# Which engine closes a one-core kernel: the gather, the semaphore clear and the last wait moved from GpSimd and SyncE to VectorE

## The chip, the cores and the metric

The kernel runs on 1 core of one Trainium2 chip. The metric is device time in microseconds (us) of one execution; medians of several runs are given. A program on one core has no second die to compare with. Unless said otherwise, the runs below are in the state that the measurements call fast; one run of the kernel before took 745.57 us, was marked slow, and is left out everywhere.

## The reference

A gated sum of two blocks for one token. Block A is grouped-query attention over a cache of 65,536 positions (32 query heads, 4 key/value heads, 128 wide), block B is a small gated MLP. Cut to what matters:

```python
q = (x @ wq).reshape(1, 1, 32, 128).transpose(0, 2, 1, 3)
k, v = jnp.repeat(k_cache, 8, axis=1), jnp.repeat(v_cache, 8, axis=1)
p = softmax(einsum('bhqd,bhkd->bhqk', q, k) * 128 ** -0.5)
a = einsum('bhqk,bhkd->bhqd', p, v).transpose(0, 2, 1, 3).reshape(1, 1, 4096) @ wo
# ... b = the MLP block ...
return g * a + (1 - g) * b            # g = sigmoid(sum(x * gate_w))
```

Only the size of the caches matters here: two times 67 MB of bfloat16 are read once. The change does not touch the arithmetic.

## The kernel before

The body streams the caches and weights through one buffer with DMAs on SyncE's queue, computes under them, and ends with one copy on ScalarE and two output DMAs, one issued by ScalarE and one by SyncE:

```python
    # ... all loads, attention, projection ...
    nc.scalar.copy(out=out_sb[:], in_=out_ps[:])
    for i, queue in enumerate((nc.scalar, nc.sync)):
        p0 = (2 * i + 1) * B - 1
        ins = queue.dma_start(out=out_rows[2 * i:2 * i + 2, :], in_=out_sb[p0:p0 + 2, :])
        out_queues.append(ins.ins.name)
```

GpSimd computes only at the start (index tables, ones, two zeroed weight buffers), until about 5 us. The framework appends a closing block, and the kernel has already cut it down in a hook that edits the finished program:

```python
    def close_with_one_barrier(n):
        block = n.main_func.blocks[-1]
        # ... `by`: the block's instructions by engine ...
        for engine, l in by.items():
            kinds = [k for _, k, _ in l]
            if engine == mybir.EngineType.Pool:                   # GpSimd
                # ... assert: Drain, wait (gather), add (release), Drain, clear, Drain, 2 more ...
                drop += [l[2][0], l[6][0], l[7][0]]
                closer, gather = l[0][0], l[1][2]
                continue
            if engine == mybir.EngineType.SP:                     # SyncE
                # ... take over and drop its wait for everything ...
                l, kinds = l[1:], kinds[1:]
            assert kinds == ["InstDrain", "InstEventSemaphore"] * 2
            drop += [l[1][0], l[2][0]]
            if engine == mybir.EngineType.SP:
                closed = l[3][0]
            else:
                drop.append(l[3][0])
        # ... the output DMAs count on a semaphore of their own, `landed`;
        #     `closer` waits for everything else, `closed` waits for `landed` ...
        for i in sorted(drop, reverse=True):
            del block.instructions[i]
```

What is left: PE, ScalarE, VectorE and SyncE each drain and add one to a gather semaphore. GpSimd waits for all other work, for the four signals of the gather, drains, clears the kernel's semaphores with one instruction, and drains again. SyncE then holds the last wait: both outputs have landed.

## Time and profile before

| | before |
|---|---|
| time, median of 3 runs | 382.19 us (382.17 to 382.25) |
| profiled run: time, span of the kernel's own instructions | 382.16 us, 380.7 us |
| bytes moved, DMA rate | 162.17 MB, 426 GB/s |
| GpSimd busy | 4.4 us, all of it before 6 us |

The page of the kernel before: the span, the engines' busy time, and the line of the DMA queue that carries the loads (packets, MB, share of the time of 16 DMA engines).

```profile
span 380.7 us, 2605 instructions
PE 233.2 (61%) x1395; PEld 56.0 (15%) x800; DVE 218.5 (57%) x211; ACT 39.6 (10%) x55; POOL 4.4 (1%) x10
q1 hardware_dynamic: 3892, 162.01, 98.8%
```

No compute engine is busy over 61% of the span, and the load queue fills 98.8% of the DMA engines' time. The kernel is bound by its loads.

The end of the kernel before, from its timeline, weight loads left out (start, duration, engine, line, what; idle time before in brackets):

```profile
378.58 0.29 PE L506 MATMUL out_ps<-kv,oa 128*32 128x256 bf16 x4 [0.35 <-DMA kv<-in_A_wo_dram]
378.92 0.37 ACT L552 CAST out_sb<-out_ps 128x256 bf16<-128x256 f32 x1 [45.10 <-PE out_ps L506]
379.32 0.32 SPq L555 DMA_DIRECT2D out_dram<-out_sb  x1
379.32 0.25 ACTq L555 DMA_DIRECT2D out_dram<-out_sb  x1
```

The issue of the outputs, at 379.32, is the zero of the tables below. The timeline leaves out drains and waits of the sequencers, so the closing block does not show in it. It shows when one asks for the source line that its instructions carry (engine, operation, count; duration in ns as minimum/median/maximum; start of the first and the last; a q marks an engine's sequencer, PEldq that of PE):

```profile
L591 POOLq EVENT_SEMAPHORE  x6: 17/43/682, 376.0 to 379.9; - x6
L591 POOLq DRAIN  x3: 34/41/72, 379.4 to 380.2; - x3
L591 DVEq DRAIN  x1: 345/345/345, 369.6 to 369.6; - x1
L591 PEldq DRAIN  x1: 347/347/347, 378.6 to 378.6; - x1
L591 ACTq DRAIN  x1: 240/240/240, 379.6 to 379.6; - x1
L591 SPq DRAIN  x1: 174/174/174, 379.7 to 379.7; - x1
L591 POOLq EVENT_SEMAPHORE_RANGE_CLEAR  x1: 96/96/96, 380.1 to 380.1; - x1
L591 SPq EVENT_SEMAPHORE  x1: 17/17/17, 380.6 to 380.6; - x1
```

GpSimd (POOLq) gathers at 379.9, clears at 380.1 and begins its last drain at 380.2. SyncE's last wait is over at 380.65. VectorE has drained already at 369.6.

**After the span.** The time of the profiled run, 382.16 us, is longer than the span, 380.7 us. The trace shows no instruction after the span, but it records semaphore updates with their times. On semaphore 2 there are two groups of nine updates; from shortly before the end of the first group until the second, nearly all of the others (246 are recorded in the kernel before) are updated once, in five groups of consecutive numbers (7 to 53, 54 to 104, 105 to 155, 156 to 206, 207 to 255). I read the two groups of nine as barriers and the updates between them as a reset, all three the runtime's, since no instruction in the trace names semaphore 2. These are names for updates: what makes them, and what values they set, is not shown. In the kernel before (us from the span's start):

```
output semaphore, last update 380.619;  SyncE's wait ends 380.653
first barrier   379.178 380.015 380.758 380.802 380.825 | 380.922 380.961 380.995 381.042
reset           380.951 to 381.604
second barrier  381.919 381.953 381.992 382.035 382.058 | 382.157 382.195 382.229 382.276
```

The second barrier takes 382.276 - 381.919 = 0.357 us, in steps of 0.023 to 0.099. The first takes longer: its second to third update needs 0.743 us, where the second barrier needs 0.039. Which engine it waits for there is the question of the experiments.

These updates are tied to the metric: the time of the profiled run equals the sixth update of the second barrier (382.16 and 382.157). So what delays these updates delays the time. Why the time ends at that update is not shown.

### The profile page before, as it was taken

The numbers are of one execution on the slowest core, as the hardware profiler recorded it, in microseconds if no ns is written. First come the engines' busy times: TensorE is split into PE (matmuls) and PEld (weight loads), VectorE is DVE, ScalarE is ACT, GpSimd is POOL, SyncE is SP. The second block draws the span as 40 slices with busy tenths as digits, with TensorE's granted clock in tenths as the row PEclk, the third lists the DMA queues.
The fourth block names the chain that finished last, engine by engine and source line by source line (L and its number), as shares of the span: only waits on it lengthen the run. The fifth ranks groups of instructions, "written<-read, shape, count | busy, mean of one in ns | idle before, by whom it ended". The sixth has DMA issues, their size and how long they took to land.

```text
span 380.7 us, 2605 instructions
## 1 busy us (share of the span) xinstructions
PE 233.2 (61%) x1395; PEld 56.0 (15%) x800; DVE 218.5 (57%) x211; ACT 39.6 (10%) x55; POOL 4.4 (1%) x10
## 2 busy tenths in 40 slices
PE   0060657876157944796397729871977196839386
PEld 0010101111101210111011101120211011202113
DVE  4133288997597506966977059669970388460040
ACT  1001001110601100114010001050100000500000
POOL 4000000000000000000000000000000000000000
PEclk9995769899759895989688958895989579969789
DMA  9998999999999999999999999999999999999995
GB/s 386 496 420 379 411 438 441 437 483 430 387 420 441 441 436 441 427 441 441 434 436 441 441 427 434 406 423 441 434 434 429 420 441 442 436 410 430 424 443 223
DMA packets 3943, 162.17 MB, mean 426 GB/s; under 512 B 472, under 2 KB 476, under 8 KB 860
## 3 DMA queue, kind: packets, MB, share of 16 engines
q1 hardware_dynamic: 3892, 162.01, 98.8%
q8 instruction: 8, 0.13, 0.1%
q14 instruction: 3, 0.02, 0.0%
q10 hardware_dynamic: 40, 0.01, 0.0%
HBM read 162.01 MB, written 0.00 MB: 426 GB/s over the span
## 4 chain that ended last, share of the span: by engine, by line
DMA 57%; PE 26%; DVE 13%; ACT 2%; issue 1%; SPq 1%; DVEq 0%; ACTq 0%
DMA kv<-in_A_k_cache_dram 43%; PE s_ps L410 21%; DMA kv<-in_A_wo_dram 7%; DVE kv L403 7%; DMA kv<-in_A_v_cache_dram 7%; PE o_ps L456 4%; DVE pt L446 2%; DVE o_sb L470 1%; DVE mx L405 1%; ACT sc L421 1%; ACT sc L443 1%; DVE rowt L466 1%; SPq L184 1%; PE om_ps L476 0%; DVE osum L486 0%
## 5 line engine op out<-in xcount | busy, mean ns | idle before, releaser
L410 PE MATMUL s_ps<-kv,wt 128*128 128x512 bf16 x512 | 141.8, 437 | 80.2 <-DVE kv L403 80.2
L403 DVE STREAM_TRANSPOSE kv<-kv 128x2048 int32<-128x2048 int32 x64 | 142.7, 2281 | 54.3 <-DMA kv<-in_A_k_cache_dram 54.3
L456 PE MATMUL o_ps<-kv,pt 128*64 128x512 bf16 x512 | 61.7, 400 | 7.6 <-DMA kv<-in_A_v_cache_dram 7.6
L410 PEld LDWEIGHTS <-wt 128*128 128x128 bf16 x256 | 27.6, 108 | 195.6 <-issue 138.5
L421 ACT CAST sc<-s_ps 128x1024 bf16<-128x1024 f32 x16 | 16.2, 1012 | 249.9 <-PE s_ps L410 249.9
L456 PEld LDWEIGHTS <-pt 128*64 128x64 bf16 x256 | 16.1, 115 | 50.6 <-issue 48.1
L446 DVE STREAM_TRANSPOSE pt<-sc 128x1024 bf16<-128x1024 bf16 x16 | 18.6, 1217 | 6.8 <-ACT sc L443 6.8
L405 DVE TENSOR_REDUCE mx<-sc 128x1 f32<-128x1024 bf16 x12 | 14.5, 1210 | 9.9 <-ACT sc L421 9.9
L443 ACT ACTIVATE sc<-sc,nb 128x1024 bf16<-128x1024 bf16 x16 | 18.2, 1137 | 12.3 <-DVE nb L439 12.2
L466 DVE TENSOR_TENSOR rowt<-o_ps,own 128x1024 f32<-128x1024 f32 x4 | 4.8, 1195 | 24.9 <-PE o_ps L456 24.9
L476 PE MATMUL om_ps<-o_sb,hsel 128*32 128x128 f32 x8 | 2.3, 386 | 18.3 <-DVE o_sb L470 18.3
L425 DVE TENSOR_REDUCE mx<-sc 128x1 f32<-128x1024 bf16 x4 | 4.9, 1220 | 13.6 <-ACT sc L421 13.6
L296 PE MATMUL q_ps<-kv,xT 128*32 128x512 bf16 x64 | 5.6, 527 | 7.2 <-DMA kv<-in_A_wq_dram 7.2
L252 PE MATMUL xb_ps<-xg,spread 8*128 8x256 bf16 x1 | 0.4, 366 | 13.2 <-DMA xg<-in_gate_w_dram 13.2
L470 DVE TENSOR_REDUCE o_sb<-rowt 128x128 f32<-128x1024 f32 x4 | 7.5, 1872 | 0.1
L363 DVE TENSOR_TENSOR rowt<-q_ps,own_b 128x512 f32<-128x512 f32 x2 | 1.3, 686 | 10.8 <-PE q_ps L296 10.8
L296 PE MATMUL z_ps<-kv,xT 128*32 128x448 bf16 x64 | 5.9, 560 | 0.0
L495 PE MATMUL busy_ps<-wt 128*128 128x512 bf16 x23 | 5.8, 381 | 0.1
L506 PE MATMUL out_ps<-kv,oa 128*32 128x256 bf16 x128 | 4.2, 274 | 2.0 <-DMA kv<-in_A_wo_dram 2.0
L256 DVE TENSOR_TENSOR xm<-xb_ps,sel_i 128x128 f32<-128x128 f32 x2 | 0.5, 287 | 8.0 <-PE xb_ps L252 8.0
L552 ACT CAST out_sb<-out_ps 128x256 bf16<-128x256 f32 x1 | 0.4, 372 | 45.1 <-PE out_ps L506 45.1
L296 PEld LDWEIGHTS <-xT 128*32 128x32 bf16 x64 | 2.6, 136 | 14.6 <-issue 14.6
(90 smaller groups left out, 59.3 us busy)
## 6 DMA issues: line engine op xcount, KB each, us to landing
kv<-in_A_k_cache_dram SPq DMA_DIRECT2D x4, 4096.0 KB, 35.4
kv<-in_A_v_cache_dram SPq DMA_DIRECT2D x2, 4096.0 KB, 26.0
kv<-in_B_w_in_dram SPq DMA_DIRECT2D x1, 7168.0 KB, 19.4
kv<-in_A_wo_dram SPq DMA_DIRECT2D x1, 6144.0 KB
kv<-in_B_w_out_dram SPq DMA_DIRECT2D x1, 3584.0 KB
kv<-in_A_wo_dram SPq DMA_DIRECT2D x1, 1024.0 KB
kv<-in_A_wo_dram SPq DMA_DIRECT2D x1, 512.0 KB
kv<-in_A_wo_dram SPq DMA_DIRECT2D x2, 256.0 KB, 28.2
```

The lines of the kernel that those rows point to most:

```text
L296: ins = nc.tensor.matmul(ps[t * B:(t + 1) * B, k * HN:k * HN + n], lhsT=xT[:, i * KH + c:i * KH + c + 1].to_broadcast([P, B]), rhs=w[:, c, ...
L403: nc.vector.transpose(out=kb[:, v * n:(v + 1) * n], in_=kb[:, v * n:(v + 1) * n])
L405: nc.vector.reduce_max(**late.pop())
L410: ins = nc.tensor.matmul(s_ps[:, k * HN:(k + 1) * HN], lhsT=wt[g % 2][:, v, b].rearrange("p a v h -> p (a v h)"), rhs=kx[:, b // 2, b % 2, ...
L421: nc.scalar.copy(out=sct[g, j][:], in_=s_ps[:])
L425: nc.vector.reduce_max(**late.pop())
L443: nc.scalar.activation(out=sct[g, j][:], in_=sct[g, j][:], func=ACT.Exp, scale=SCALE, bias=nb[:, 0:1], accum_out=lss[g][:, j:j + 1])
L446: nc.vector.transpose(out=ptt[g, j][:].rearrange("p c x -> p (c x)"), in_=sct[g, j][:])
L456: ins = nc.tensor.matmul(o_ps[g][hs, e, :], lhsT=ptt[g, j][:, 2 * u:2 * u + 2, :].rearrange("p c x -> p (c x)"), rhs=vx[:, 2 * u + e], sta ...
L466: nc.vector.tensor_tensor(out=om8, in0=o_ps[g][:].rearrange("p e (v d) -> p (e v) d", d=DH), in1=own_8[:].unsqueeze(2).to_broadcast([P, 2 ...
L470: nc.vector.tensor_reduce(out=o_sb[:], in_=om8.rearrange("p x d -> p d x"), axis=AX.X, op=ALU.add)
L495: ins = nc.tensor.matmul(ps[:, :HN], lhsT=w[:, :P], rhs=w[:, :HN], start=True, stop=True, skip_group_check=True)
```

## The change

The intent: VectorE, idle for over nine microseconds by then, should gather, clear and hold the last wait, so that GpSimd's program is over after its set-up work. The hook keeps one of GpSimd's own two last instructions as the last wait, lets SyncE go after its drain, and then swaps GpSimd and VectorE in the closing block.

```diff
-                drop += [l[2][0], l[6][0], l[7][0]]
-                closer, gather = l[0][0], l[1][2]
+                drop += [l[2][0], l[6][0]]
+                closer, gather, closed = l[0][0], l[1][2], l[7][0]
                 continue
             ...
             assert kinds == ["InstDrain", "InstEventSemaphore"] * 2
-            drop += [l[1][0], l[2][0]]
-            if engine == mybir.EngineType.SP:
-                closed = l[3][0]
-            else:
-                drop.append(l[3][0])
+            drop += [l[1][0], l[2][0], l[3][0]]
         ...
         for i in sorted(drop, reverse=True):
             del block.instructions[i]
+        swap = {mybir.EngineType.Pool: mybir.EngineType.DVE,
+                mybir.EngineType.DVE: mybir.EngineType.Pool}
+        for i, ins in enumerate(block.instructions):
+            if ins.engine in swap:
+                block.instructions[i] = copy.replace(ins, engine=swap[ins.engine])
```

## The prediction

> **What bounds the kernel.** The page gives DMA 98.8% of 16 engines' span on the main queue, 426 GB/s; the table by stretches has the DMA engines at 99 to 100% from 0 to 365 us. It streams 162 MB. The change touches none of that: it rewrites only the closing block, after the last load. In the listing of instructions by engine only the semaphore clear moves, from GpSimd to VectorE.
>
> **The end of the kernel before** (timeline, and the closing line's instructions, us from the span's start). The last matmuls run at 378.58, the output copy at 378.92 for 0.37 us, both output DMAs issue at 379.32. ScalarE's closing drain ends at 379.86, SyncE's at 379.87. GpSimd gathers at 379.89, drains, clears the semaphores at 380.08 (0.10 us), and ends its last drain at 380.23. The outputs' landings, in the trace's semaphore records, end at 380.62; SyncE's last wait ends at 380.65, and the span is 380.7. So GpSimd's gather and clear (about 0.35 us) already lie in the shadow of the output landing, which needs about 1.3 us from issue.
>
> **What the change does.** VectorE's last arithmetic ends at about 369.9, so it is free to gather. The waits, gather and clear move to it; it then holds the wait for the outputs. [...] The span therefore stays 380.7.
>
> **Where something can be won or lost.** The time (382.16 in the profiled run) is longer than the span: after it come the runtime's barrier, a semaphore reset and another barrier, which the trace shows as updates only. The first barrier's updates come at 379.18, 380.02, 380.758, 380.802, 380.825, then back to 381.04. I read these as PE, ACT, GpSimd, VectorE, SyncE in turn (an inference: engines start the kernel in the reverse order after the same barrier). If so GpSimd arrives 0.52 us after its last drain and is the one the barrier waited for; SyncE would have been ready about as soon. Freeing GpSimd early takes this away, but VectorE, fourth in turn, then arrives only after the landing: 380.65 plus its own way into the barrier. ScalarE needed 0.16 us for that way, PE 0.23; with 0.1 to 0.2 for VectorE the fifth update comes at 380.78 to 380.88 against 380.825. That is -0.05 to +0.05 us.
>
> **Prediction.** 382.17 us, 8 in 10 between 381.8 and 382.6, a width mostly for run-to-run differences of DMA timing. Faster by over 2%: 0.003. Within 2%: 0.992. Slower by over 2%: 0.005.
>
> **What would show it right or wrong.** Right: the span 380.7 within 0.3; the closing waits, drains and clear appear on VectorE, over by about 380.3; the last instruction is VectorE's wait, at the landing; GpSimd's last instruction is at about 5 us; the third barrier update follows the second at once, and the fourth comes 0.1 to 0.2 us after VectorE's wait. Wrong: VectorE's chain ending after the landing, or its way into the barrier taking 0.3 us or more.
>
> **What would make it wrong.** The order of engines in the barrier, or the cause of the third update's lateness, is other than I read it; the clear costs far more on VectorE than 0.1 us; GpSimd's early end starts something in the runtime that collides with the loads.

## The result

| | before | changed |
|---|---|---|
| median of 6 runs | 382.18 us (381.99 to 382.25) | 382.24 us (382.11 to 382.49) |
| profiled run, time and span | 382.16, 380.7 us | 382.24, 380.8 us |

The ratio is 1.0003, with a 95% interval of 0.999 to 1.0016: the same. A ratio is the mean time of one kernel's fast runs over that of the other's of the same rounds, so it is not quite the ratio of these medians.

The changed kernel's page, the same three lines:

```profile
span 380.8 us, 2607 instructions
PE 231.3 (61%) x1397; PEld 55.6 (15%) x800; DVE 218.5 (57%) x211; ACT 39.6 (10%) x55; POOL 4.4 (1%) x10
q1 hardware_dynamic: 3892, 162.01, 98.8%
```

The load queue's line is the same, and VectorE, ScalarE and GpSimd are as busy as before. PE's busy time is 1.9 us lower, at a granted clock of 0.852 instead of 0.839 in this run; the kernel waits for its loads all the same. The end of its timeline, weight loads left out:

```profile
378.70 0.29 PE L507 MATMUL out_ps<-kv,oa 128*32 128x256 bf16 x4 [0.35 <-DMA kv<-in_A_wo_dram]
379.04 0.37 ACT L553 CAST out_sb<-out_ps 128x256 bf16<-128x256 f32 x1 [45.48 <-PE out_ps L507]
379.44 0.33 SPq L556 DMA_DIRECT2D out_dram<-out_sb  x1
379.44 0.26 ACTq L556 DMA_DIRECT2D out_dram<-out_sb  x1
```

In this run the stream happened to end 0.12 us later. This is the spread that has to be taken out: in the eleven traces of whole kernels, the issue of the outputs falls anywhere from 379.32 to 379.63. The prediction had named one way in which the change could reach the stream, GpSimd's early end. The three traces in which GpSimd ends early have the issue at 379.33, 379.44 and 379.63, the eight others at 379.32 to 379.60, so nothing points to it. The changed closing line:

```profile
L592 DVEq EVENT_SEMAPHORE  x7: 21/50/672, 376.1 to 380.8; - x7
L592 DVEq DRAIN  x3: 10/10/17, 379.5 to 380.3; - x3
L592 POOLq DRAIN  x1: 4111/4111/4111, 1.0 to 1.0; - x1
L592 PEldq DRAIN  x1: 347/347/347, 378.7 to 378.7; - x1
L592 ACTq DRAIN  x1: 241/241/241, 379.7 to 379.7; - x1
L592 SPq DRAIN  x1: 165/165/165, 379.8 to 379.8; - x1
L592 DVEq EVENT_SEMAPHORE_RANGE_CLEAR  x1: 120/120/120, 380.2 to 380.2; - x1
```

All of it now stands on VectorE (DVEq). GpSimd's one closing drain starts at 1.0 us and lasts 4.1 us, until its last memset is done (5.06 us); it then has nothing left. The updates after it:

```
output semaphore, last update 380.743;  VectorE's wait ends 380.791
first barrier   379.389 380.141 380.179 380.967 380.990 | 381.089 381.127 381.161 381.208
second barrier  381.995 382.029 382.068 382.112 382.135 | 382.234 382.272 382.306 382.353
```

Counted from the issue of the outputs, in us:

| | before | changed |
|---|---|---|
| last engine of the gather has cleared and drained | 0.914 (GpSimd) | 0.882 (VectorE) |
| outputs landed | 1.299 | 1.303 |
| last wait ends | 1.333 (SyncE) | 1.351 (VectorE) |
| second update of the first barrier | 0.695 | 0.701 |
| third | 1.438 | 0.739 |
| fourth | 1.482 | 1.527 |
| fifth | 1.505 | 1.550 |
| last update of the second barrier | 2.956 | 2.913 |

The third update came 0.70 us earlier, as it should if GpSimd had been the one that came late. The fourth now waits, and the fifth is 0.045 us later than before. But the last line has the opposite sign: from the end of the first barrier to the start of the second it took 0.877 us in the profile of before and 0.787 in that of the changed kernel. That needed an experiment too.

### The profile page after: what moved, and what is told of

The parts are those of the page before. It is cut to its first block, busy times and chain, and to the rows that moved or that the text cites. A ratio compares the mean times of both kernels' runs of the same rounds, so it can differ in the third digit from the quotient of the medians.

```text
span 380.8 us, 2607 instructions
## 1 busy us (share of the span) xinstructions
PE 231.3 (61%) x1397; PEld 55.6 (15%) x800; DVE 218.5 (57%) x211; ACT 39.6 (10%) x55; POOL 4.4 (1%) x10
## 3 DMA queue, kind: packets, MB, share of 16 engines
q1 hardware_dynamic: 3892, 162.01, 98.8%
## 4 chain that ended last, share of the span: by engine, by line
DMA 57%; PE 24%; DVE 15%; issue 2%; ACT 2%; SPq 1%; DVEq 0%; ACTq 0%
DMA kv<-in_A_k_cache_dram 42%; PE s_ps L411 19%; DVE kv L404 8%; DMA kv<-in_A_wo_dram 7%; DMA kv<-in_A_v_cache_dram 7%; PE o_ps L457 4%; DVE pt L447 2%; DVE mx L406 1%; DVE o_sb L471 1%; ACT sc L422 1%; ACT sc L444 1%; DVE rowt L467 1%; SPq L185 1%; PE om_ps L477 0%; DVE osum L487 0%
## 5 line engine op out<-in xcount | busy, mean ns | idle before, releaser
L411 PE MATMUL s_ps<-kv,wt 128*128 128x512 bf16 x512 | 139.0, 428 | 82.4 <-DVE kv L404 82.3
```

The source lines that it names most:

```text
L411: ins = nc.tensor.matmul(s_ps[:, k * HN:(k + 1) * HN], lhsT=wt[g % 2][:, v, b].rearrange("p a v h -> p (a v h)"), rhs=kx[:, b // 2, b % 2, ...
```

## The experiments

Theory: the runtime's barrier is entered in the order PE, ScalarE, GpSimd, VectorE, SyncE. Each engine has its own way from its last instruction into the barrier, and GpSimd's is 0.52 us. The change takes away GpSimd's late arrival and puts VectorE's in its place. Rivals: the third in the order is SyncE (in the changed kernel both GpSimd and SyncE end early, so the two traces alone cannot say); the long way belongs to the drain and clear and not to GpSimd; or nothing here counts but the landing of the outputs.

Eight variants were run in two groups, each with runs of the kernel before on the same chip (382.18 us median for the first four, 382.25 for the last four). All eight gave correct results. All eight are the same as before at 2%, and the 95% interval of the ratio includes 1 for each: differences of times below are only a support, and the updates carry the argument. All times in the tables are from the issue of the outputs.

### VectorE gathers and clears, SyncE keeps the last wait (e1_sync_holds)

```diff
 # the kernel before, plus:
+        swap = {mybir.EngineType.Pool: mybir.EngineType.DVE,
+                mybir.EngineType.DVE: mybir.EngineType.Pool}
+        for i, ins in enumerate(block.instructions):
+            if ins.engine in swap:
+                block.instructions[i] = copy.replace(ins, engine=swap[ins.engine])
```

> Half of the change alone: VectorE gathers and clears, GpSimd ends early, but SyncE keeps the last wait as before. Theory (the runtime's barrier is entered in the order PE, ScalarE, GpSimd, VectorE, SyncE, and GpSimd's way into it takes 0.52 us after its last instruction): the third and fourth updates follow the second within 0.05 us each, at about 380.1, and only the fifth waits, for SyncE's own way after its wait; it comes at most 0.17 us after that wait's end, so issue to fifth update is 1.43 to 1.50 us against 1.505 before and 1.550 after. Rival (third in the order is SyncE, not GpSimd): the third update waits for the landing and comes about 0.1 us after SyncE's wait, the fifth 0.067 us later. Total time under both: within 0.15 us of before, too small to tell them apart; the updates decide.

Its closing line, on the two engines in question:

```profile
L596 DVEq DRAIN  x3: 10/10/17, 379.7 to 380.5; - x3
L596 POOLq DRAIN  x1: 4106/4106/4106, 1.0 to 1.0; - x1
L596 DVEq EVENT_SEMAPHORE_RANGE_CLEAR  x1: 120/120/120, 380.3 to 380.3; - x1
L596 SPq EVENT_SEMAPHORE  x1: 17/17/17, 380.9 to 380.9; - x1
```

The third update follows the second by 0.039 us although SyncE waits until 1.333: SyncE is not third. The fifth comes at 1.474, 0.141 us after SyncE's wait, so SyncE is fifth. One detail of the expectation was wrong: the fourth update does not follow the third at once but comes at 1.013, 0.131 us after VectorE's last drain. I had forgotten that VectorE still gathers here. It has slack, so nothing came of it. With this way SyncE would have come at about 1.474 in the kernel before as well, so at the fifth update GpSimd's late arrival had cost only 0.03 us there. The step from the fifth to the sixth update took 0.045 us here, against 0.097 to 0.099 in the two kernels above, and this makes up the larger part of the gain. The step is short in the traces where the fifth update waits for SyncE (here, in e6_pool_no_clear and in s3); why is not shown. The last update of the second barrier came at 2.784, against 2.956 before and 2.913 changed. The time was 382.14 us (382.00 to 382.40), ratio 0.9998 with an interval of 0.9985 to 1.0012: the gain is too small for whole runs of this kernel.

### GpSimd gathers, clears and holds (e2_pool_holds)

```diff
 # the changed kernel, less its swap:
-        swap = {mybir.EngineType.Pool: mybir.EngineType.DVE,
-                mybir.EngineType.DVE: mybir.EngineType.Pool}
-        for i, ins in enumerate(block.instructions):
-            if ins.engine in swap:
-                block.instructions[i] = copy.replace(ins, engine=swap[ins.engine])
```

> The change without its swap: GpSimd gathers, clears and holds the last wait. Theory (GpSimd is third and needs 0.52 us from its last instruction into the barrier): the wait ends about 0.03 us after the landing, the third update comes 0.5 us after that, issue to fifth update is about 1.92 us, and the time is 0.35 to 0.45 us longer than before. Rival one (SyncE is third, GpSimd fifth with a way as short as the others'): third and fourth updates early, the fifth 0.1 to 0.2 us after the wait, issue to fifth update 1.45 to 1.55, time as before. Rival two (the 0.52 us is the way of a drain and clear, not of GpSimd as such): third update 0.1 to 0.2 us after the wait, time as before.

Of its closing line:

```profile
L587 POOLq EVENT_SEMAPHORE  x7: 17/43/682, 376.0 to 380.6; - x7
L587 POOLq DRAIN  x3: 34/41/72, 379.4 to 380.2; - x3
L587 SPq DRAIN  x1: 177/177/177, 379.7 to 379.7; - x1
L587 POOLq EVENT_SEMAPHORE_RANGE_CLEAR  x1: 96/96/96, 380.1 to 380.1; - x1
```

GpSimd's wait ends at 1.335, as SyncE's did before, and the third update comes at 1.896, 0.561 us after it. The fifth is at 1.963 instead of 1.505. The time is 382.63 us (382.55 to 382.80) against 382.18: 0.45 longer, and the two sets of runs (before: 382.12 to 382.47) do not overlap, although the recorded interval of the ratio, 0.9999 to 1.0024, still touches 1. Both rivals fall: GpSimd is third, and its way is over half a microsecond even when its last instruction is a bare wait.

### Is there slack in the gather and clear? (e4_pool_three_clears, e5_vector_three_clears)

The clear is issued three times, on GpSimd in the kernel before and on VectorE in the changed one:

```diff
+        at = next(i for i, ins in enumerate(block.instructions) if type(ins).__name__ == "InstISA")
+        clear = block.instructions[at]
+        for k in range(2):
+            block.instructions.insert(at + 1, copy.replace(clear, name=f"I-{90001 + k}"))
```

> The kernel before with the semaphore clear on GpSimd issued three times. Theory (before, GpSimd's way sets the barrier's third update, so its chain has no slack beyond some 0.05 us): the chain ends about 0.25 us later (two clears at 0.125 us from start to start), near 380.5, the third update comes about 0.25 us later, issue to fifth update rises from 1.505 to about 1.75, time plus 0.25 us. Rival (the gather and clear are hidden under the output landing, which SyncE waits for until 380.65): nothing moves, issue to fifth update stays at 1.50.

> The changed kernel with the clear on VectorE issued three times. Theory: the chain ends about 0.3 us later, near 380.62, still ahead of the landing at about 380.75, VectorE's wait and everything after it stay: issue to fifth update 1.55, time as in the changed kernel. Rival (the clear on VectorE costs more than its record shows, or is on the path): issue to fifth update rises by 0.1 to 0.3 us.

Lines of the closing, on GpSimd, and then on VectorE:

```profile
L595 POOLq EVENT_SEMAPHORE_RANGE_CLEAR  x3: 90/90/96, 380.3 to 380.5; - x3
L595 SPq EVENT_SEMAPHORE  x1: 17/17/17, 380.8 to 380.8; - x1
```

```profile
L596 DVEq EVENT_SEMAPHORE_RANGE_CLEAR  x3: 107/107/114, 380.1 to 380.3; - x3
L596 DVEq EVENT_SEMAPHORE  x7: 21/49/672, 376.0 to 380.7; - x7
```

On GpSimd the chain ended at 1.150, still before SyncE's wait ended (1.333), and yet the third update moved from 1.438 to 1.675 and the fifth to 1.741. The time was 382.44 us (382.41 to 382.52), 0.26 above the same rounds' 382.18 (382.12 to 382.47). Within the span these clears look hidden under the landing; they are not, because 0.52 us of GpSimd's way still follow. On VectorE the same lengthening did nothing: fifth update 1.553 against 1.550, time 382.19 us.

### The other half of the change alone (e3_vector_holds)

```diff
-            if engine == mybir.EngineType.SP:
+            if engine == mybir.EngineType.DVE:
                 closed = l[3][0]
```

> The other half of the change alone: GpSimd gathers and clears as before, VectorE holds the last wait in place of SyncE. Theory: GpSimd makes the third update come about 1.44 us after the issue, as before; VectorE's way after its wait (0.18 us in the changed kernel) makes the fourth about 1.52, so the fifth comes at about 1.55 us, as in the changed kernel: what the change costs up to there is VectorE's way alone. Rival (the cost came with the gather and clear on VectorE): fifth update at 1.50, as before. Time within 0.15 us of before.

```profile
L591 DVEq EVENT_SEMAPHORE  x1: 21/21/21, 380.9 to 380.9; - x1
```

The third update is where it was (1.440), the fourth comes 0.196 us after VectorE's wait, and the fifth at 1.565. Holding the wait on VectorE by itself therefore gives what the whole change gives (1.550). The gain of moving the gather is lost behind it. The time was 382.27 us (382.25 to 382.42).

### The clear left out (e6_pool_no_clear)

```diff
-                drop += [l[2][0], l[6][0], l[7][0]]
+                drop += [l[2][0], l[3][0], l[4][0], l[6][0], l[7][0]]
```

> The kernel before without the kernel's own semaphore clear and the drain ahead of it [...]. GpSimd's chain ends about 0.2 us earlier. Theory: the third update moves earlier by about 0.2 us, to 1.24 us after the issue; the fifth then waits for SyncE alone and comes 1.43 to 1.50 us after the issue, a gain of at most 0.07 us. Rival (SyncE is third in the order): third update unmoved at 1.44.

```profile
L591 POOLq DRAIN  x2: 34/38/41, 379.5 to 380.1; - x2
```

The third update came at 1.217, 0.22 us earlier, and the fifth at 1.476, 0.141 us after SyncE's wait: the same end as in e1_sync_holds by another road. The step from the fifth to the sixth was again short (0.044), and the last update came at 2.787. The time was 382.16 us (382.00 to 382.22).

### The wait on ScalarE and on PE (e7_scalar_holds, e8_tensor_holds)

The same one-line edit as in e3_vector_holds, with ScalarE and with PE.

> The kernel before with the last wait on ScalarE in place of SyncE. Theory (ScalarE is second): second update 0.16 us after the wait's end, about 1.49 us after the issue, third 0.04 later unless GpSimd is later still, fifth at about 1.60 us; time plus 0.1 us. Rival (the holder does not matter, what counts is the landing): fifth at 1.50 to 1.51.

> The kernel before with the last wait on TensorE. Theory (TensorE is first, its way 0.23 us): first update 0.23 us after the wait's end, four further steps of together about 0.15 us, fifth update at about 1.73 us after the issue; time plus 0.2 us. Rival (the holder does not matter): fifth at 1.50 to 1.51.

The last wait, in the first run and in the second:

```profile
L591 ACTq EVENT_SEMAPHORE  x1: 17/17/17, 380.7 to 380.7; - x1
L591 PEldq EVENT_SEMAPHORE  x1: 51/51/51, 380.7 to 380.7; - x1
```

| who holds the last wait, and who gathers | first update that waits for it | way into the barrier | fifth update | time, and before's in the same rounds |
|---|---|---|---|---|
| PE (GpSimd gathers) | first | 0.239 | 1.767 | 382.50, 382.25 |
| ScalarE (GpSimd gathers) | second | 0.139 | 1.585 | 382.36, 382.25 |
| GpSimd (GpSimd gathers) | third | 0.561 | 1.963 | 382.63, 382.18 |
| VectorE (VectorE gathers: the change) | fourth | 0.176 | 1.550 | 382.24, 382.18 |
| SyncE (GpSimd gathers: before) | none: the third waits for GpSimd | - | 1.505 | 382.19 |
| SyncE (VectorE gathers) | fifth | 0.141 | 1.474 | 382.14, 382.18 |

The first five updates of the barrier in the same six traces, from the issue; the jump to the holder moves along the row (in the row of before the jump at the third is GpSimd's):

```
PE                         1.627  1.661  1.699  1.743  1.767
ScalarE                   -0.143  1.479  1.517  1.561  1.585
GpSimd                    -0.142  0.697  1.896  1.940  1.963
VectorE (the change)      -0.051  0.701  0.739  1.527  1.550
SyncE (before)            -0.142  0.695  1.438  1.482  1.505
SyncE (VectorE gathers)   -0.142  0.700  0.739  1.013  1.474
```

Each holder shows at its own place in the order, which turns the order from an inference into an observation. The holder does matter, by its way and by how many steps follow it. In the times it shows less surely: 382.23 to 382.50 with ScalarE and 382.41 to 382.98 with PE, against before's 382.12 to 382.30.

### The second barrier's late start (b2_before_again)

The kernel before, unchanged.

> The kernel before, unchanged, for a second profile. In its first one, first to second barrier took 0.877 us from the last update of one to the first of the other, where the changed kernel and all eight variants took 0.785 to 0.790. Theory (an accident of that one run): 0.785 to 0.79 here, issue to last update 2.87. Rival (it belongs to this closing): 0.88 again, 2.96. Issue to fifth update 1.50 under both.

It took 0.788 us from the first barrier's last update to the second's first, like the changed kernel and the eight variants (0.785 to 0.790); fifth update 1.510, last update 2.872. So the 0.877 us do not belong to this closing. Against this undisturbed trace the changed kernel's 2.913 is 0.041 later, and e1_sync_holds' 2.784 is 0.088 earlier. The two profiled runs even had their outputs issued within 0.004 us of each other (379.444 and 379.440), and their times are 382.20 for before and 382.24 for the change. Why the first profile of before started its second barrier late stays open. The reset in between took the same time in both (0.65 us); the delay lies after its last update, 0.315 us from there to the second barrier instead of 0.224.

### The closing on a short kernel (s1, s2, s3)

To lose the spread of the stream, three kernels kept only half of one weight's load, the set-up, and the output; their results are wrong.

```diff
-    win = load(win_view, (KC, F), 3)
-    ...                                   # wq, and everything after the constants
+    win = load(win_view[:, :KH, :], (KH, F), 3)
+    ...
+    out_ps = win[:, 0, :NO]
```

> Wrong result on purpose: the kernel before with its stream taken out. It loads half of one weight (3.67 MB), sets up its constants on GpSimd and VectorE, copies a corner of the load and writes it out, and closes as the kernel before does; about 10 to 20 us, so the run-to-run spread of the long stream (0.1 us) should be gone and a few hundredths of a microsecond count. This is the base for the next two. Issue to fifth update 1.50 us, issue to last barrier update 2.87 us (2.96 if the second barrier is late again, as it was in the profile of before alone).

> The same short kernel with the changed closing (wrong result on purpose). Theory: the change costs 0.045 us, VectorE's way into the barrier after the landing (issue to fifth update 1.55 us, to the last update 2.91), so the time is 0.03 to 0.06 us above the short kernel before. Rival (the lateness of the second barrier in the profile of before, 0.09 us, belongs to that closing and the change removes it): 0.03 to 0.06 us below.

> The same short kernel with VectorE gathering and clearing and SyncE holding the last wait (wrong result on purpose). Theory: issue to fifth update 1.475 us and to the last update 2.785, 0.08 us under the short kernel before and 0.13 under the short changed one, in the time as well. Rival (the gain seen in two traces is an accident of alignment): within 0.02 us of the short kernel before.

| | short before | short changed | short, SyncE holds |
|---|---|---|---|
| outputs issued at | 11.570 | 11.458 | 11.730 |
| fifth update, from the issue | 1.502 | 1.547 | 1.467 |
| last update, from the issue | 2.908 | 2.957 | 2.819 |
| time, median and range | 14.36 (14.34 to 14.37) | 14.34 (14.30 to 14.37) | 14.27 (14.22 to 14.43) |

From the issue on, the differences are those of the long kernel: +0.049 and -0.089 us. (All three last updates come some 0.04 us later than expected: between the barriers it took 0.83 us here instead of 0.79, for a reason not looked for.) In the time they do not come out safely: s2 was expected 0.03 to 0.06 above s1 and its median lies 0.02 below; s3's median lies 0.09 below, as expected, but its runs reach from 14.22 to 14.43. In the profiled runs the outputs were issued up to 0.27 us apart; even a short load varies by more than what was to be measured. As tests of the whole time these three are inconclusive.

A better use of whole runs is the time less the span, which leaves the stream out (spans are given to 0.1 us, so single values can be off by 0.05). For the kernel before, its 24 fast runs of the three groups average 1.45 us, none below 1.38. For e1_sync_holds, whose span ends with the same wait on SyncE, five runs average 1.32, none above 1.35. For e6_pool_no_clear, which ends nearly alike, four average 1.36, one of them at 1.47. So that gain, about 0.1 us, is seen in the runs and not only in one trace. Three of before's values lie at 1.54 and 1.55, where its undisturbed trace has 382.20 - 380.78 = 1.42; that is more than rounding explains, so a late barrier as in the first profile probably comes now and then, and lifts the mean (an inference: there is no trace of these runs). For the changed kernel six runs average 1.46, with a span that itself ends 0.014 us later after the landing (0.048 against 0.034 in the profiled runs). By the same measure the three short kernels do separate, in the order that their updates give: 1.46 (1.44 to 1.47) before, 1.51 (1.47 to 1.54) changed, 1.35 (1.32 to 1.38) with SyncE holding.

## Why the prediction was right

- **The body is bound by loads and is untouched: right.** DMA share (98.8%) and mean rate (426 GB/s) are the same.
- **The span stays, with the chain on VectorE hidden under the landing: right.** The chain was over at 0.882 us after the issue, the landing came at 1.303. The prediction had the chain over by about 380.3, 0.98 us after the issue at 379.32. From the gather's last wait to the end of the last drain it took 0.30 us, where GpSimd's took 0.34 before. By instruction it went both ways in these two traces: VectorE's clear took 120 ns against GpSimd's 96, its shortest waits 21 against 17, but its drains after the gather and after the clear took 10 and 10 ns against 72 and 34. In the three-clear runs the clear's median is 107 ns against 90.
- **The barrier's order and GpSimd as the late one: right,** and no longer an inference. (The inference was from the start of the trace of before: nine updates on semaphore 2 from 0.375 to 0.004 us ahead of the span, and then the first recorded instructions of SyncE at 0.000, VectorE 0.120, GpSimd 0.130, ScalarE 0.139 and PE 0.312.) With the last wait on PE, ScalarE, GpSimd, VectorE or SyncE, the first, second, third, fourth or fifth update waits.
- **VectorE's way takes the gain back: right.** Predicted -0.05 to +0.05 us at the fifth update; measured +0.045 (+0.040 against the second profile of before), near the edge of the range. I allowed 0.1 to 0.2 us for VectorE's way; it was 0.176. (PE's way, 0.23 in the prediction, reads 0.244 in the trace; nothing rests on it.)
- **382.17 us against 382.24 measured.** The number tested little: the median of the kernel before lies in the predicted range as well, so no part of the mechanism was needed to meet it. What tested the mechanism were the updates. The change's own part of the difference of 0.07 is 0.04 by the traces; the rest can't be told from the spread. The two kernels' ranges overlap, so not even the sign is shown by the medians alone. It is shown from the issue of the outputs on.
- **What the prediction missed** is that the same idea without its second half is better: with SyncE holding, both late arrivals are avoided (fifth update at 1.474, against 1.505 before and 1.550 changed).

Why GpSimd needs over half a microsecond is not shown: the trace has no instructions after the span. That it does so after a drain (0.524 to 0.526 in five full-length traces), after a wait (0.561), and with or without the clear, is.

## What to carry to other kernels

In this program the last instruction in the profile was not the end of the time (380.7 us of 382.16): the engine that held the last wait took 0.14 to 0.56 us more into the runtime's barrier. Work that looked hidden under a later wait inside the span was exposed after it: with three clears on GpSimd the chain was over at 1.150 us, before SyncE's wait ended at 1.333, and the fifth update still moved from 1.505 to 1.741. It was best to let GpSimd finish early and to give the last wait to SyncE, which is last in the barrier's order and has a short way (0.141 us); even that gains only 0.09 us of 382. Moving the late arrival from GpSimd to VectorE made the third update 0.70 us earlier and the fifth 0.045 us later, because VectorE's own way (0.176 us) came after the landing. Effects of this size had to be read inside one trace from a fixed event: the issue of the outputs alone fell anywhere from 379.32 to 379.63 us.
